# Output of tiles 3 to 6 on three pairs of half-filled banks, with attention running on into it, and a second set of temporaries

## The chip, the cores and the metric

One core of one Trainium2 chip. The metric is device time in microseconds (us). The kernel before took 848.38 us (median of 3 runs, 846.76 to 848.47).

## The reference

Attention within chunks of 64 tokens, for 8 batches, 8 heads and 576 tokens of 64 values, and behind it a two-layer feed-forward network with a quadratic ReLU:

```python
scores = scale * np.matmul(q_c, k_c.transpose(0, 1, 2, 4, 3))
scores = scores - np.max(scores, axis=-1, keepdims=True)
attn = np.exp(scores)
attn = attn / (np.sum(attn, axis=-1, keepdims=True) + 1e-09)
out = np.matmul(attn, v_c)
...
h = x @ w_in
g = np.where(pos, h, np.where(neg, 0.0, (h + beta) ** 2 / (4.0 * beta)))
return (g @ w_out).astype(np.float32)
```

x has 4608 tokens of 512 values, w_in is 512 x 2048 and w_out 2048 x 512, all in float32.

## The kernel before, in words

The tokens are cut into 9 tiles of 512. Every float32 operand of a matmul is split into a high and a low part of a rounded type (F32R), and a product is taken as three: high by high, high by low, low by high.

Tiles 0 to 2 run as plain products (`ffn_in`, line 607, and `ffn_out`, line 643), 16 steps a tile. While they run, two other things are made for the tiles behind them. `combine_weights` makes, for each of 8 pairs of blocks of w_in, the sums of a Strassen scheme with seven products, and `combine_out` does the same for w_out. Both work in four temporaries named `tmp`; from there the sums go to DRAM as `combos` (line 826) and `sums` (line 974) over the queue of GpSimd (POOL). The lists `WEIGHTS` and `SUMS_AT` say at which step of tiles 1 and 2 each pair has its turn; three pairs of w_out are not in the list, and `combine_out` is called for them while tiles 3 and 4 already run.

Tiles 3 to 8 run two at a time, as 3 and 4, 5 and 6, 7 and 8, each pair of tiles in two halves. In the hidden half, `whole_last` runs 56 products (`product`, line 891) of 6 matmuls of 512 columns, on the PSUM banks h0, h1, o0 and o1. In the output half, `both_out` runs 7 rounds, P1, P2, P6, P7, P4, P5, P3, of 8 products each (line 1101). A product there covers four blocks of 128 tokens. Before the change, each block has a bank for itself: rounds P1, P6, P4 and P3 take the banks o2, o3 and the pair `ps_a`, the other rounds take h0, h1, o0 and o1. The rounds in `wide` (P1, P6 and P4) make high by both halves of the factor in one matmul of 512 columns and add a second one of 256, 8 matmuls in all; the two halves of the bank are added when it is read. The other rounds use three matmuls of 256 columns per block, 12 in all. For the last pair of tiles nothing of this is changed.

Each product takes its weights from a ring of tiles in SBUF, `RING` places of 256 KB, which POOL's queue fills in the order of use (lines 864 and 869). A place is filled again when its product is done.

Attention of the later tiles is cut into 36 turns, 4 a tile. A burst is the value products of turn n and the score products of turn n + 2 (lines 487 and 465), both on the bank pair `ps_a`. Between them lies the softmax of the turn: VectorE (DVE) takes the maximum (line 521), ScalarE (ACT) the exponentials (line 530), DVE the division and a transposition (line 570), and eight small DMAs, four on SP's and four on POOL's queue, bring the result to `aT` (line 562), which the value products read two bursts later. `BURSTS` says before which of the 56 products of a hidden half a burst is placed. q, k and v of later turns are loaded over SP's queue (lines 382 and 398).

The order on each engine is not that of the code. `Plan` collects all operations with an estimated duration, and places them by readiness and turn; each engine then works its list in order and waits where an operand is late. So a late operand holds back what stands behind it on the same engine.

Of the kernel before, what the change touches and what calls it, by code (L numbers as in the profile page):

```python
# [133 lines left out]
def kernel(  # L134
# [540 lines left out]
    RING = 12  # L675
# [106 lines left out]
    def combine_weights(p):  # L782
        js = (2 * p, 2 * p + 1)
        keys = [[f"wi{j}_{n}" for n in range(2)] for j in js]
        (k1, w1), (k12, s12), (k2, w2), (k34, s34) = tmp_bufs

        def kc(ap):
            return ap.rearrange("p (i two f) -> p two i f", i=2, two=2)

        def two(ap, n):  # L790
            return ap[:, cols(n)].rearrange("p (i f) -> p i f", i=2)

        for j, ks, key, w in zip(js, keys, (k1, k2), (w1, w2)):
            dve(0.6, ALU.add, fixed(w), lambda j=j: weight["wi", j][:, 0, :].bitcast(F32),
                lambda j=j: weight["wi", j][:, 1, :].bitcast(F32), ks, (key,))
        a11, a12, a21 = kc(w1)[:, 0], kc(w1)[:, 1], kc(w2)[:, 0]
        a22 = kc(w2)[:, 1]
        dve(0.34, ALU.add, fixed(two(s12, 0)), fixed(a21), fixed(a22), (k2,), (k12,))
        dve(0.34, ALU.subtract, fixed(two(s12, 1)), fixed(two(s12, 0)), fixed(a11), (k1,), (k12,))
        dve(0.34, ALU.subtract, fixed(two(s34, 0)), fixed(a11), fixed(a21), (k1, k2), (k34,))  # L800
        dve(0.34, ALU.subtract, fixed(two(s34, 1)), fixed(a12), fixed(two(s12, 1)), (k1, k12), (k34,))
        for hkey, hi, key, ap in ((k1, w1, k12, s12), (k2, w2, k34, s34)):
            act_copy(0.52, fixed(hi.bitcast(F32R)), fixed(ap), (key,), (hkey,))
            dve(0.6, ALU.subtract, fixed(ap.bitcast(F32R)), fixed(ap), fixed(hi), (hkey,), (key,))
# [7 lines left out]
        def of_stage(n, h):  # L812
            return lambda: tmp_pairs[n][:, :, cols(h)].rearrange("p x (i f) -> p x i f", i=2)

        for r, src, reads in (
            (0, of_block(0, 0), (*keys[0], k12)), (1, of_block(0, 1), (*keys[0], k12)),
            (6, of_block(1, 1), (*keys[1], k12)),
            (2, of_stage(0, 1), st[0]), (3, of_stage(0, 0), st[0]),
            (5, of_stage(1, 0), st[1]), (4, of_stage(1, 1), st[1]),
        ):  # L820
# [117 lines left out]
    BURSTS = range(2, 46, 6)  # L938
# [17 lines left out]
    def combine_out(p):  # L956
        js = (2 * p, 2 * p + 1)
        keys = [[f"wo{j}_{n}" for n in range(2)] for j in js]
        (k1, w1), (k12, s12), (k2, w2), (k34, s34) = tmp_bufs
        for j, ks, key, w in zip(js, keys, (k1, k2), (w1, w2)):  # L960
            dve(0.6, ALU.add, fixed(w), lambda j=j: weight["wo", j][:, 0, :].bitcast(F32),
                lambda j=j: weight["wo", j][:, 1, :].bitcast(F32), ks, (key,), ahead=LATER)
        a11, a21, a12, a22 = (fixed(w[:, cols(n)]) for w in (w1, w2) for n in range(2))
        s1, s2, s3, s4 = (fixed(w[:, cols(n)]) for w in (s12, s34) for n in range(2))
# [4 lines left out]
        for hkey, hi, key, ap in ((k1, w1, k12, s12), (k2, w2, k34, s34)):  # L969
            act_copy(0.52, fixed(hi.bitcast(F32R)), fixed(ap), (key,), (hkey,), ahead=LATER)  # L970
            dve(0.6, ALU.subtract, fixed(ap.bitcast(F32R)), fixed(ap), fixed(hi), (hkey,), (key,), ahead=LATER)
        for n, name in enumerate(SUMS):
            def send(n=n, name=name):
                nc.gpsimd.dma_start(
                    out=sums[name, p].bitcast(F32), in_=tmp_pairs[n // 2][:, :, cols(n % 2)]
# [73 lines left out]
    def both_out(t, wide, then=None):  # L1049
# [8 lines left out]
        banks = {name: main if name in ("P1", "P6", "P4", "P3") else side for name in OUT_ORDER}  # L1058
        alone = ("P1", "P2", "P7", "P5", "P3")
# [11 lines left out]
        def operand_of(name, p):  # L1071
# [4 lines left out]
            act_copy(0.52, h, ap, (skey,), (hkey,))  # L1076
            dve(0.6, ALU.subtract, l, ap, plain(h), (skey, hkey), (lkey,))
# [35 lines left out]
        def pairs_of(name, half):  # L1113
            if banks[name] is side:
# [156 lines left out]
    def back(t, g):  # L1271
# [11 lines left out]
        ("x0",), ("x1",), ("x2",), ("x3", "x4"), ("x5", "x6"), ("x7", "x8"), ("x9", "x10"),  # L1283
        ("x11", "ring1"), ("ring2", "ring3"),
# [8 lines left out]
    SUMS_AT = (0, 16, 18, 20, 23)  # L1293
    WEIGHTS = (2, 4, 7, 9, 12, 14, NF + 10, NF + 12)
# [17 lines left out]
    for t in range(ALONE + 1):  # L1312
        for j in range(NF):
# [17 lines left out]
            if step in WEIGHTS:  # L1331
                combine_weights(WEIGHTS.index(step))
            if step in SUMS_AT:
                combine_out(SUMS_AT.index(step))
# [4 lines left out]
            if t == ALONE and j < len(HANDED):  # L1339
                hand_lot("wi", j, F32R, *HANDED[j])  # L1340
# [13 lines left out]
    for n, (key, _) in enumerate((*gh_bufs, *gl_bufs)):  # L1354
        take(f"ring_{key}", key, [P, T], F32R, (key,), (f"ring_{key}",))

    turns = [(n, n + 2) for n in range((ALONE + 3) * NP, ALL - 2)] + [(ALL - 2, None), (ALL - 1, None)]
    for t in range(ALONE + 1, NTILE, 2):
        if t > ALONE + 1:
            move_blocks()  # L1360
        for n, (p, name) in enumerate(alternating(0, NQ)):
            if n in BURSTS and turns:
                burst(*turns.pop(0))
# [73 lines left out]
```

## Time and profile before

| | |
|---|---|
| median of 3 runs | 848.38 us |
| the profiled execution | 848.42 us |
| its span, first to last instruction | 846.6 us |
| TensorE (PE) busy | 816.9 us, 96% |
| DVE busy | 665.0 us, 79% |
| ACT busy | 540.2 us, 64% |
| mean granted TensorE clock | 0.988 |

PE is busy nearly all the time, so what is of interest is where it is not, and where its clock is not full. The span lies in these stretches: tiles 0 to 2 up to about 327 us, the hidden half of tiles 3 and 4 to about 433, their output half to 518, the hidden half of tiles 5 and 6 to about 602 and their output half to 681, and the last pair of tiles to the end.

### The profile page before, as it was taken

How to read it: one execution, taken by the hardware profiler on the slowest of the kernel's cores; microseconds unless marked ns; L12 is line 12 of the kernel's file. 1: busy time of each engine (PE TensorE's matmuls, PEld its weight loads, DVE VectorE, ACT ScalarE, POOL GpSimd, SP SyncE). 2: the span in 40 equal slices, each digit the busy share in tenths (PEclk: the TensorE clock that was granted, in tenths of full speed). 3: DMA queues.
4: the chain of work that ended last, by engine and by line, in shares of the span. 5: the costliest groups of instructions: out<-in, count | busy, mean ns of one | idle time of the engine just before them, and what ended most of it. 6: DMA issues, size and time to landing. Idle time of an engine off the chain costs nothing.

```text
span 846.6 us, 18141 instructions
## 1 busy us (share of the span) xinstructions
PE 816.9 (96%) x6272; PEld 692.0 (82%) x6272; DVE 665.0 (79%) x1163; ACT 540.2 (64%) x1299; POOL 343.6 (41%) x606
## 2 busy tenths in 40 slices
PE   8999999999999999888699999999999999999998
PEld 8877788888878888666579999777899998888887
DVE  4999997877988885967489976867898755579962
ACT  5789885556676674857495545877855446677440
POOL 2233334354443554645343333545433334333330
PEclk9999999999999999989799999999999999999999
DMA  9999946676786997999986668986667675566762
GB/s 226 246 299 295 290 129 197 177 235 188 191 226 152 244 250 218 257 223 251 225 229 184 209 210 236 257 233 206 185 197 198 209 237 196 191 194 188 213 194 93
DMA packets 245354, 181.58 MB, mean 214 GB/s; under 512 B 192656, under 2 KB 210576, under 8 KB 245264
## 3 DMA queue, kind: packets, MB, share of 16 engines
q0 software_dynamic: 40640, 122.72, 46.0%
q1 hardware_dynamic: 202512, 57.18, 29.7%
q8 instruction: 50, 0.82, 0.4%
q10 hardware_dynamic: 2112, 0.52, 0.3%
q14 instruction: 40, 0.33, 0.1%
HBM read 133.17 MB, written 38.80 MB: 203 GB/s over the span
## 4 chain that ended last, share of the span: by engine, by line
PE 54%; DMA 8%; DVE 3%; ACT 3%; issue 2%; SPq 2%; POOL 0%; DVEq 0%; ACTq 0%; POOLq 0%
PE ps_o L1101 14%; PE ps_o L891 9%; PE ps_a L1101 8%; PE ps_h L891 7%; PE ps_h L1101 6%; PE ps_o L643 5%; PE ps_h L607 4%; DMA k_sb<-in_k_dram 2%; ACT e L530 1%; DMA sums_P<-tmp 1%; DVE new_wi L922 1%; SPq L382 1%; DMA v_sb<-in_v_dram 1%; PE ps_a L487 1%; DMA aT<-e 1%
## 5 line engine op out<-in xcount | busy, mean ns | idle before, releaser
L607 PE MATMUL ps_h<-xh,parts 128*128 128x512 f32 x384 | 130.0, 397 | 2.3 <-DVE parts L350 1.7
L724 ACT CAST new_wi<-new_wi 128x512 fp32r<-128x512 f32 x146 | 89.3, 620 | 67.0 <-PE ps_o L1101 34.6
L728 DVE TENSOR_TENSOR new_wi<-new_wi,new_wi 128x512 fp32r<-128x512 f32 (+1 forms) x186 | 120.3, 683 | 13.1 <-ACT new_wi L724 12.6
L643 PE MATMUL ps_o<-parts,gh 128*128 128x512 f32 x384 | 118.7, 390 | 0.4 <-DVE tmp L657 0.4
L607 PEld LDWEIGHTS ps_h<-xh,parts 128*128 128x128 f32 x384 | 71.9, 188 | 19.1 <-DVE parts L350 2.6
L643 PEld LDWEIGHTS ps_o<-parts,gh 128*128 128x128 f32 x384 | 71.8, 188 | 15.7 <-DVE tmp L657 0.8
L643 PE MATMUL ps_o<-parts,gl 128*128 128x512 f32 x192 | 74.8, 390 | 0.7 <-DVE gl L628 0.7
L864 POOL DMA_DIRECT2D new_wi<-sums_P x84 | 45.0, 536 | 68.2 <-PE ps_a L1101 28.9
L869 POOL DMA_DIRECT2D new_wi<-combos x84 | 45.4, 542 | 66.2 <-PE ps_o L891 27.6
L562 POOL DMA_DIRECT2D aT<-e x96 | 48.3, 511 | 50.6 <-issue 15.8
L1101 PE MATMUL ps_o<-new_wi,new_wi 128*128 128x256 f32 (+1 forms) x380 | 68.0, 309 | 0.0
L922 DVE SCALAR_TENSOR_TENSOR new_wi<-h,new_wi 128x512 f32<-128x512 f32 x62 | 41.9, 684 | 25.1 <-ACT new_wi L921 25.0
L891 PE MATMUL ps_o<-new_wi,new_wi 128*128 128x512 f32 x234 | 60.2, 399 | 0.0
L1101 PEld LDWEIGHTS ps_o<-new_wi,new_wi 128*128 128x128 f32 x380 | 53.9, 190 | 4.1
L530 ACT ACTIVATE e<-ps_a,mx 128x64 f32<-128x64 f32 x168 | 49.9, 325 | 8.8 <-DVE mx L526 6.2
L918 ACT ACTIVATE new_wi<-h 128x512 f32<-128x512 f32 x62 | 39.4, 638 | 21.5 <-DVE h L912 21.5
L891 PEld LDWEIGHTS ps_o<-new_wi,new_wi 128*128 128x128 f32 x234 | 44.2, 192 | 9.8 <-ACT snaps L724 0.3
L921 ACT ACTIVATE new_wi<-new_wi 128x512 f32<-128x512 f32 x84 | 51.4, 633 | 1.1
L607 PE MATMUL ps_h<-x_parts,parts 128*128 128x512 f32 x128 | 49.9, 390 | 0.0
L626 ACT CAST gh<-r 128x512 fp32r<-128x512 f32 x48 | 30.0, 626 | 28.0 <-PE ps_o L643 14.1
L891 PE MATMUL ps_h<-new_wi,new_wi 128*128 128x512 f32 x186 | 47.7, 391 | 0.0
L487 PEld LDWEIGHTS ps_a<-aT,v_sb 64*64 64x64 f32 x1056 | 20.8, 139 | 28.0 <-issue 19.2
(238 smaller groups left out, 2088.8 us busy)
## 6 DMA issues: line engine op xcount, KB each, us to landing
new_wi<-combos POOLq DMA_DIRECT2D x84, 256.0 KB, 4.2
new_wi<-sums_P POOLq DMA_DIRECT2D x84, 256.0 KB, 3.2
words<-in_moe_w_in_dram SPq DMA_DIRECT2D x16, 512.0 KB, 7.7
words<-in_moe_w_out_dram SPq DMA_DIRECT2D x16, 512.0 KB, 6.4
sums_P<-tmp POOLq DMA_DIRECT2D x32, 256.0 KB, 4.2
combos<-tmp POOLq DMA_DIRECT2D x32, 256.0 KB, 3.6
v_sb<-in_v_dram SPq DMA_DIRECT2D x60, 128.0 KB, 4.6
q_sb<-in_q_dram SPq DMA_DIRECT2D x112, 64.0 KB, 4.3
```

The source lines that it names most:

```text
L530: nc.scalar.activation(out=e3[:, n, :], in_=sc[:, n // 4, n % 4, :], func=AF.Exp, bias=mx[:, n, :], scale=SCALE, accum_out=sm[:, n, :],)
L562: queues[queue].dma_start(out=aT[b:b + Q, to], in_=x[a:a + Q, of])
L607: nc.tensor.matmul(out=ps, lhsT=weight["wi", j][:, half, kc * P:(kc + 1) * P], rhs=x, start=(kc == 0 and i == 0), stop=(kc == KC - 1 and i ...
L643: nc.tensor.matmul(out=acc, lhsT=x[:, cols], rhs=weight["wo", j][:, half, :], start=(j == 0 and i == 0), stop=(j == NF - 1 and i == 2),)
L724: "act", cost, lambda: nc.scalar.copy(out=out(), in_=src()), reads, writes, ahead=ahead
L728: plan.add("dve", cost, lambda: nc.vector.tensor_tensor(out=out(), in0=one(), in1=two(), op=op), reads, writes, port=True, ahead=ahead)
L864: plan.add("pool", 0.55, lambda: nc.gpsimd.dma_start(out=ap().bitcast(F32), in_=sums[name, p].bitcast(F32).rearrange("p x f -> p (x f)")), ...
L869: plan.add("pool", 0.55, lambda: nc.gpsimd.dma_start(out=ap().bitcast(F32), in_=combos[d][:, n, :].bitcast(F32)), (f"dram{d}_{n}",), (key, ...
L891: nc.tensor.matmul(out=ps, lhsT=w()[:, at:at + P], rhs=y(), start=name in FRESH and i == 0 and k == 0, stop=i == 1 and k == 2, skip_group_ ...
L921: plan.add("act", 0.52, lambda: nc.scalar.square(out=now(r), in_=now(r)), (), (rkey,), ahead=50)
L922: plan.add("dve", 0.6, lambda: nc.vector.scalar_tensor_tensor(out=now(r), in0=h(), scalar=1.0, in1=now(r), op0=ALU.max, op1=ALU.min), (hke ...
L1101: nc.tensor.matmul(out=into, lhsT=x()[:, block], rhs=factor, start=first and k == 0, stop=p == NQ - 1 and k == len(steps) - 1, skip_group_ ...
```

## The change

In the output halves of tiles 3 to 6 no round is wide. Two blocks of 128 tokens share a bank, each on 256 of its 512 columns, so that a round needs two banks. The rounds go over three pairs of banks: (o2, o3), (h0, h1) and (o0, o1). The pair `ps_a` is left to attention.

`BURSTS` places a burst every 9 products instead of every 6, and counts on into the output half: two of the eight bursts now lie there, before the fourth product of P1 and the fifth of P2.

`combine_weights` and `combine_out` can work in a second set of temporaries, `alt0` and `alt1`, which lie in the places of the first two blocks of w_in once tile 2 has used them; every second call from step 18 on uses it. Two more turns of `combine_out` are earlier: six pairs are in `SUMS_AT`, at steps 0, 6, 12, 18, 20 and 23, and two calls are left for tiles 3 and 4. In `combine_weights` the sends from the temporaries now come before those from the blocks. The ring has 10 places instead of 12; two of its pairs of places are gone and the buffers `r` take one pair's part, which come free only when tile 2's hidden layer is done.

```diff
-    RING = 12
+    RING = 10
...
+    def stage_of(again):
+        if again:
+            some = [(f"alt{n}_{i}", part_of(f"alt{n}", i)) for n in range(2) for i in range(2)]
+            return *some, [lambda n=n: held[f"alt{n}"] for n in range(2)]
+        return *((key, fixed(ap)) for key, ap in tmp_bufs), [fixed(pair) for pair in tmp_pairs]
...
-        if k >= 4:
-            key = f"ring_{(gh_bufs, gl_bufs)[n][k - 4][0]}"
+        if k >= 2:
+            key = f"ring_{(gh_bufs, gl_bufs, r_bufs)[k - 2][n][0]}"
...
-    BURSTS = range(2, 46, 6)
+    BURSTS = range(5, 72, 9)
...
+        if not last:
+            thirds = o_banks[2:], h_banks, o_banks[:2]
+            banks = {name: thirds[n] for name, n in zip(OUT_ORDER, (0, 1, 0, 2, 0, 1, 2))}
...
+            soon = 200 if name == "P1" and p < 2 else 0
...
-                    acc, block = banks[name][n][1], slice(n * P, (n + 1) * P)
+                    block = slice(n * P, (n + 1) * P)
+                    acc = banks[name][n][1] if last else banks[name][n // 2][1][:, cols(n % 2)]
...
-                        first = name in alone and p == 0
+                        first = name in alone and p == 0 and (last or n % 2 == 0)
...
+                between(len(alternating(0, NQ)) + NQ * OUT_ORDER.index(name) + p)
...
-    SUMS_AT = (0, 16, 18, 20, 23)
-    WEIGHTS = (2, 4, 7, 9, 12, 14, NF + 10, NF + 12)
+    SUMS_AT = (0, 6, 12, 18, 20, 23)
+    WEIGHTS = (2, 4, 8, 10, 14, 21, 26, 28)
+    AGAIN = sorted(step for step in (*SUMS_AT, *WEIGHTS) if step > 17)[::2]
...
+    def between(n):
+        if n in BURSTS and turns:
+            burst(*turns.pop(0))
...
-                if p % 2 and p < 2 * (NQ - len(SUMS_AT)):
-                    combine_out(len(SUMS_AT) + p // 2)
+                if p in (1, 4):
+                    combine_out(len(SUMS_AT) + p // 4, p > 1)
...
-            both_out(t, ('P1', 'P6', 'P4'), lambda raws=raws: pieces_of(raws))
+            both_out(t, then=lambda raws=raws: pieces_of(raws))
```

On PE, where tiles 3 and 4 go over from the hidden to the output half, before the change. Line 891 is a product of the hidden half, line 1101 one of the output half; `ps_o23` is the bank pair o2, o3.

```order
L891 MATMUL ps_o1_140<-new_wi2_3_2700,new_wi8_9_3154 128x512 x3
L891 MATMUL ps_o1_140<-new_wi6_7_3009,new_wi8_9_3154 128x512 x3
L1101 MATMUL ps_o23_137<-ring_gh0_3674,new_wi4_5_2873 128x512
L1101 MATMUL ps_o23_137<-ring_gh0_3674,new_wi4_5_2873 128x256
...
L1101 MATMUL ps_a_138<-ring_gh0_3674,new_wi4_5_2873 128x512
L1101 MATMUL ps_a_138<-ring_gh0_3674,new_wi4_5_2873 128x256
```

The same place after it; lines 899 and 1114 are the two lines' new numbers, 487 and 465 are a burst.

```order
L899 MATMUL ps_o_139<-new_wi_3_2703,ring_gh_3704 128x512 x3
L899 MATMUL ps_o_139<-new_wi_7_3031,ring_gh_3704 128x512 x3
L899 MATMUL ps_o_140<-new_wi_5_2891,ring_gh_3733 128x512 x3
L899 MATMUL ps_o_140<-new_wi_9_3187,ring_gh_3733 128x512 x3
L1114 MATMUL ps_o_137<-ring_r_3681,new_wi_4_2817 128x256 x12
L487 MATMUL ps_a<-aT_78,v_sb_72 64x64 x16
L465 MATMUL ps_a<-kT_75,qT_74 64x64 x16
L1114 MATMUL ps_o_137<-ring_r_3693,new_wi_7_3031 128x256 x12
```

A product of P1 was eight matmuls of two widths on four banks and is now twelve of 256 columns on two banks, and a burst on `ps_a` stands between two of them.

On POOL's queue, at the start of the hidden half of tiles 3 and 4, before the change; line 869 fills a place of the ring, line 974 sends sums of a pair (here pair 5) from `tmp` to DRAM, line 562 moves attention weights.

```order
L869 DMA new_wi_9_3154<-combos_109 128x512
L562 DMA aT_78<-e_76 32x256 x4
L869 DMA ring_gh_3674<-combos_112 128x512
L974 DMA sums_P_5_193<-tmp_135 256x1x256
L869 DMA ring_gl_3675<-combos_110 128x512
L974 DMA sums_P_5_169<-tmp_135 256x1x256
L869 DMA ring_gh_3703<-combos_111 128x512
L869 DMA ring_gl_3704<-combos_112 128x512
L974 DMA sums_P_5_177<-tmp_136 256x1x256
L974 DMA sums_P_5_201<-tmp_136 256x1x256
```

After it, from the last sends of tile 2 on; line 982 is 974's new number, 877 that of 869, and `new_wi_0` and `new_wi_1` are the second set of temporaries.

```order
L982 DMA sums_P_7_195<-new_wi_0_2541 256x1x256
L982 DMA sums_P_7_171<-new_wi_0_2541 256x1x256
L982 DMA sums_P_7_179<-new_wi_1_2611 256x1x256
L982 DMA sums_P_7_203<-new_wi_1_2611 256x1x256
L562 DMA aT_78<-x_80 32x256 x4
L562 DMA aT_79<-e_77 32x256 x4
L877 DMA ring_r_3681<-combos_104 128x512
L877 DMA new_wo_2_2729<-combos_107 128x512
L877 DMA ring_r_3693<-combos_105 128x512
L877 DMA ring_gh_3704<-combos_104 128x512
L877 DMA ring_gl_3705<-combos_105 128x512
```

Twelve sends of sums (pairs 5, 6 and 7) stood among the ring's fills of this half. Now those of pairs 5 and 7 stand ahead of its fills, and the four of pair 6 come some twenty rows further down.

## Rows read from the trace of the kernel before

**Rows 1.** The page: head.

```profile
span 846.6 us, 18141 instructions
```

**Rows 2.** Four stretches: length, PE, PEld, DVE, ACT, POOL busy, PEclk, DMA share, GB/s.

```profile
222.00:327.00 105.00, 104.61 (x927) 85.14 (x926) 88.67 (x175) 70.04 (x220) 47.39 (x81) 1.00 0.81 209
327.00:433.00 106.00, 89.28 (x825) 71.71 (x824) 75.22 (x146) 71.75 (x224) 52.66 (x96) 0.90 0.95 246
433.00:518.00 85.00, 84.31 (x595) 78.84 (x595) 75.65 (x128) 48.01 (x85) 31.82 (x61) 1.00 0.68 200
518.00:602.00 84.00, 81.80 (x763) 65.66 (x762) 59.69 (x108) 63.34 (x186) 40.35 (x77) 1.00 0.85 233
```

**Rows 3.** Waits of PE, 327 to 433 us: total, times, longest.

```profile
PE ps_a L487 <- DMA aT<-e: 9.4, 2, 7.7
PE ps_a L487 <- DMA aT<-x: 3.8, 1, 3.8
PE ps_a L487 <- DMA q_sb<-in_q_dram: 1.0, 1, 1.0
PE ps_h L891 <- DVE new_wi L922: 0.9, 1, 0.9
PE ps_h L891 <- DVE h L912: 0.8, 1, 0.8
PE ps_o L891 <- DVE new_wi L922: 0.8, 1, 0.8
```

**Rows 4.** Stretches of one burst and three products each, columns as in Rows 2.

```profile
371.82:377.09 5.27, 5.27 (x84) 4.22 (x82) 5.00 (x10) 4.95 (x21) 4.87 (x9) 1.00 1.04 237
363.92:371.82 7.90, 7.90 (x82) 6.62 (x83) 3.28 (x7) 2.38 (x5) 0.57 (x1) 0.66 0.68 143
387.31:395.38 8.07, 7.27 (x83) 5.83 (x83) 7.13 (x13) 5.01 (x20) 3.25 (x7) 0.79 0.82 217
415.56:423.18 7.62, 7.62 (x82) 6.44 (x83) 2.56 (x5) 1.81 (x3) 1.11 (x2) 0.68 0.60 115
```

**Rows 5.** The chain of waits, 340 to 440 us: start, length, what.

```profile
349.05 5.71 DMA sums_P<-tmp
354.76 0.71 ACT e L530 x5
...
359.25 4.42 DMA aT<-x
...
363.92 1.39 PE ps_a L487 x29
```

**Rows 6.** DMA queues and two issue lines, 327 to 433 us.

```profile
q0 software_dynamic: 6031, 17.56, 51.8%
q1 hardware_dynamic: 44331, 8.34, 42.7%
...
sums_P<-tmp POOLq DMA_DIRECT2D x12, 256.0 KB, 6.2
...
new_wo<-combos POOLq DMA_DIRECT2D x7, 256.0 KB, 6.8
```

**Rows 7.** Rounds P6 and P5 of tiles 3 and 4, and 40 us around.

```profile
460.68:471.98 11.30, 11.30 (x66) 9.80 (x65) 11.30 (x21) 6.00 (x10) 4.29 (x8) 1.00 0.79 229
494.81:506.32 11.51, 11.51 (x98) 11.51 (x97) 10.87 (x19) 6.00 (x10) 4.29 (x8) 1.00 0.77 231
440.00:480.00 40.00, 40.00 (x277) 37.17 (x277) 40.00 (x70) 24.19 (x42) 15.21 (x29) 1.00 0.69 197
```

**Rows 8.** Waits of PE, 518 to 602 us: total, times, longest.

```profile
PE ps_a L487 <- ACT snaps L724: 1.3, 1, 1.3
PE ps_a L487 <- DMA aT<-e: 0.4, 1, 0.4
PE ps_o L891 <- DVE new_wi L922: 0.3, 1, 0.3
```

**Rows 9.** A group by line, DVE, 327 to 433 us: busy us, mean ns.

```profile
L521 DVE TENSOR_REDUCE mx<-ps_a 128x8 f32<-128x512 f32 x8 | 5.5, 686 | 11.5 <-ACT more L724 7.9 <-PE ps_a L465 3.6
```

More of the change, by code (lines that the diff above doesn't have):

```diff
@@ L793, in combine_weights @@
         for j, ks, key, w in zip(js, keys, (k1, k2), (w1, w2)):
-            dve(0.6, ALU.add, fixed(w), lambda j=j: weight["wi", j][:, 0, :].bitcast(F32),
+            dve(0.6, ALU.add, w, lambda j=j: weight["wi", j][:, 0, :].bitcast(F32),
                 lambda j=j: weight["wi", j][:, 1, :].bitcast(F32), ks, (key,))
-        a11, a12, a21 = kc(w1)[:, 0], kc(w1)[:, 1], kc(w2)[:, 0]
-        a22 = kc(w2)[:, 1]
-        dve(0.34, ALU.add, fixed(two(s12, 0)), fixed(a21), fixed(a22), (k2,), (k12,))
@@ L799, in combine_weights @@
-        dve(0.34, ALU.subtract, fixed(two(s12, 1)), fixed(two(s12, 0)), fixed(a11), (k1,), (k12,))
-        dve(0.34, ALU.subtract, fixed(two(s34, 0)), fixed(a11), fixed(a21), (k1, k2), (k34,))
-        dve(0.34, ALU.subtract, fixed(two(s34, 1)), fixed(a12), fixed(two(s12, 1)), (k1, k12), (k34,))
+        a11, a12, a21, a22 = (kc(w, n) for w in (w1, w2) for n in range(2))
+        dve(0.34, ALU.add, two(s12, 0), a21, a22, (k2,), (k12,))
+        dve(0.34, ALU.subtract, two(s12, 1), two(s12, 0), a11, (k1,), (k12,))
@@ L954, in keep_factor, with combine_out @@
                  moving=0.8, ahead=LATER)
-    def combine_out(p):
+    def combine_out(p, again=False):
         js = (2 * p, 2 * p + 1)
         keys = [[f"wo{j}_{n}" for n in range(2)] for j in js]
-        (k1, w1), (k12, s12), (k2, w2), (k34, s34) = tmp_bufs
+        (k1, w1), (k12, s12), (k2, w2), (k34, s34), pairs = stage_of(again)
         for j, ks, key, w in zip(js, keys, (k1, k2), (w1, w2)):
-            dve(0.6, ALU.add, fixed(w), lambda j=j: weight["wo", j][:, 0, :].bitcast(F32),
+            dve(0.6, ALU.add, w, lambda j=j: weight["wo", j][:, 0, :].bitcast(F32),
                 lambda j=j: weight["wo", j][:, 1, :].bitcast(F32), ks, (key,), ahead=LATER)
-        a11, a21, a12, a22 = (fixed(w[:, cols(n)]) for w in (w1, w2) for n in range(2))
-        s1, s2, s3, s4 = (fixed(w[:, cols(n)]) for w in (s12, s34) for n in range(2))
+        a11, a21, a12, a22 = (part(w, n) for w in (w1, w2) for n in range(2))
+        s1, s2, s3, s4 = (part(w, n) for w in (s12, s34) for n in range(2))
         dve(0.34, ALU.add, s1, a21, a22, (k1, k2), (k12,), ahead=LATER)
@@ L974, in send @@
                 nc.gpsimd.dma_start(
-                    out=sums[name, p].bitcast(F32), in_=tmp_pairs[n // 2][:, :, cols(n % 2)]
+                    out=sums[name, p].bitcast(F32), in_=pairs[n // 2]()[:, :, cols(n % 2)]
                 )
@@ L1047, in take_low, with both_out @@
         plan.add("pool", 0.0, emit, (), (key,))
-    def both_out(t, wide, then=None):
+    def both_out(t, wide=(), then=None):
         last = then is None
@@ L1113, in pairs_of @@
         def pairs_of(name, half):
+            if not last:
+                return [((key,), lambda ap=ap: ap.rearrange("p (n d) -> p n d", n=2), b, None)
+                        for b, (key, ap) in enumerate(banks[name])]
             if banks[name] is side:
@@ L1331 @@
             if step in WEIGHTS:
-                combine_weights(WEIGHTS.index(step))
+                combine_weights(WEIGHTS.index(step), step in AGAIN)
             if step in SUMS_AT:
-                combine_out(SUMS_AT.index(step))
+                combine_out(SUMS_AT.index(step), step in AGAIN)
             if t == 0 and j >= 8:
@@ L1339 @@
             if t == ALONE and j < len(HANDED):
-                hand_lot("wi", j, F32R, *HANDED[j])
+                hand_lot("wi", j, F32 if j < 2 else F32R, *HANDED[j])
                 if j == 2:
@@ L1361 @@
         for n, (p, name) in enumerate(alternating(0, NQ)):
-            if n in BURSTS and turns:
-                burst(*turns.pop(0))
+            between(n)
             if t == ALONE + 1 and name == "P1":
-                if p % 2 and p < 2 * (NQ - len(SUMS_AT)):
-                    combine_out(len(SUMS_AT) + p // 2)
+                if p in (1, 4):
+                    combine_out(len(SUMS_AT) + p // 4, p > 1)
                 place_blocks(p)
```

38 lines of the change are left out of this document (21 added, 17 removed).

## The prediction

> **What bounds the kernel now.** I read the page's head first, then a table of stretches, then PE's waits in the stretch that stands out, then the chain of waits there. The span is 846.6 us [rows 1], and the profiled execution took 848.42 us, so 1.8 us lie around the span; the median of the runs is 848.38 us, so what is summed against the profiled execution holds for the median as well.
>
> The table of stretches [rows 2] shows a PE that is full in the tiles before (104.61 of 105 us) and in the output half of tiles 3 and 4 (84.31 of 85), and one stretch that is not: 327 to 433 us, the hidden half of tiles 3 and 4, with 89.28 of 106 us at a mean granted clock of 0.90. It is also the stretch with the fullest DMA engines, a share of 0.95 against 0.68 behind it. So the question is what the change does to this stretch, and what it costs in the others.
>
> PE's waits there [rows 3] sum to 9.4 + 3.8 + 1.0 + 0.9 + 0.8 + 0.8 = 16.7 us, and 14.2 us of them are value products that wait for a load or for the moves of the attention weights. Behind each of the three long waits the clock is at its lower level for a while. Four stretches of equal work, a burst and three products, give its price [rows 4]: undisturbed it takes 5.27 us at clock 1.00; behind the waits it takes 7.90, 8.07 (with a wait of 0.8 in it) and 7.62 us. That is 2.6 + 2.0 + 2.4 = 7.0 us more. So this stretch loses 16.7 + 7.0 = 23.7 us, and PE's work in it is 106 - 23.7 = 82.3 us.
>
> Why are the moves late? The chain [rows 5] shows one case: a send of sums from the temporaries took 5.71 us to land, then ACT's exponentials went on, then the move took 4.42 us, and then PE started. ACT had stood still, since the next copy into those temporaries was ahead of the exponentials in its order. The queues show the wider cause [rows 6]: POOL's queue kept the 16 engines for 51.8% of 106 us, which is 54.9 us for 17.56 MB or 67 transfers of 256 KB (0.82 us each), and SP's queue for 42.7%, which is 45.3 us for 8 turns of attention (5.7 us each). Together 100.2 us of transfers against 82.3 us of PE work: the stretch asks for more than its length.
>
> The Trainium skill (Trainium Kernel Development and Optimization, Key Constraints) says that DMAs from the SP, ACT and POOL queues all run on the same 16 engines. By that rule the two shares add up, as I do here; if each queue had engines of its own, neither 54.9 nor 45.3 us would fill 82.3 us, and the waits would have to be latency. The trace agrees with the rule in so far as the mean share of 0.95 is their sum.
>
> **The change part by part.**
>
> *Fewer transfers beside tiles 3 and 4's hidden half.* Of the 12 sends of sums [rows 6] four are left there, by the order on POOL's queue: 8 x 0.82 = 6.6 us less. Two of eight bursts move to the output half: 2/8 x 45.3 = 11.3 us less. That leaves 100.2 - 6.6 - 11.3 = 82.3 us, by chance just PE's work. The move of a turn also gets more time: it is read two bursts later, and two bursts were 12 products apart and are now 18; at about 1.4 us a product (a round of eight takes 11.30 us [rows 7]) that is 25 us instead of 17. And the sums of pair 7 use the second temporaries, so the pattern of the chain can come up once, not three times. What stays lost: nothing as the lower bound; as the upper bound of this mechanism, 82.3 us of transfers at the rate that the full stretch had, 100.2 us in 106, take 87.1 us, 4.8 us over PE's work. The stretch 518 to 602 us, with a DMA share of 0.85 on the mean, still loses 2.0 us [rows 8]. I take 4, near the upper end, since the load is uneven within the stretch: 23.7 - 4 = 19.7 us gained.
>
> *Tiles 5 and 6's hidden half.* The same spacing, with 2.0 us to gain at most [rows 8]; I take 1.0.
>
> *No wide rounds.* A wide round of 8 products takes 11.30 us and one of 12-matmul products 11.51 us, both with PE full [rows 7]: 0.21 us a round, and six rounds change (P1, P6, P4, twice), so 1.3 us more, on PE's path and hidden by nothing. The weights of a product are loaded beside the matmul before; in the row of 12 matmuls the loads are as long as PE (11.51 of 11.51 us), which is why more of them show.
>
> Of this the Trainium skill (TensorE: Matmul & The Clock Gate, Back-to-back issue gap) gives about 2.5 ns of fixed cost for each further matmul; an estimate from that is 192 more matmuls x 2.5 ns = 0.5 us. The rows say 1.3 us, and the measurement decides; the forecast would be 0.8 us lower by the Trainium skill.
>
> *Reading the banks.* Six times two adds of 128x512 on DVE go, three times per output half. They stood beside PE's next round, so they free DVE and no time on PE's path by themselves.
>
> *Attention in the output half.* DVE is the engine to watch: 40.00 of 40 us between 440 and 480 us [rows 7], with PE full only because DVE's splits run some products ahead. A turn's softmax costs DVE five instructions of the size of the maximum, which takes 0.69 us [rows 9]: 3.5 us, so two turns bring 6.9 us; the four adds of P1 and P6 that go in that span take 2.8 us away. Net 4.1 us in a stretch where DVE has no gap. What covers it: after 484 us DVE has room (75.65 of 85 us in the whole half [rows 2]). If the lead is used up, PE waits for at most these 4.1 us; if it is not, nothing. In tiles 5 and 6 the two bursts there have no scores any more, so no softmax. I take 1.5 us, nearer to nothing, since PE waits there only once before. PE queues nothing else behind such a wait that could go on.
>
> *The ring's 10 places.* A load starts 10 products ahead, some 14 us, and the slowest kind lands within 6.8 us on the median in the full stretch [rows 6]. At the start of the stretch six of the places come free only with the end of tile 2's work, but four products are loaded before. The bound is one late load at each of the three starts, 0 to 3 us. The two earlier turns of `combine_out` and the shifted ones of `combine_weights` go into tiles 1 and 2, where PE had no wait and DVE 88.67 of 105 us [rows 2]; one more set of some 4 us fits. Both together: 0 to 4 us, I take 0.5.
>
> *The sum:* -19.7 - 1.0 + 1.3 + 1.5 + 0.5 = -17.4 us, 848.4 - 17.4 = 831 us.
>
> **The rivals.**
>
> 1. *The DMA engines still bound the stretch.* The 82.3 us of transfers are just PE's work, so any that I counted too low, or the pair's four sends together with the ring's first fills, bring back waits of several us, each with its slow clock behind it. For it speaks that the share is 0.95 with no slack; against it that 518 to 602 us loses little at 0.85. With half of the loss left, 11.9 us: 831 + 7.9 = 839 us.
>
> 2. *Everything goes.* No wait is left in either hidden half and DVE's lead holds: 848.4 - 23.7 - 2.0 + 1.3 = 824 us. For it speaks that the three long waits hang on single late moves; against it that short waits for DVE [rows 3] are no matter of DMA.
>
> 3. *Slower: the wait is the softmax's way through three engines in order, not traffic.* Then each burst waits as before wherever it stands, 23.7 us stay lost, and the two that move into the output half take their waits along (16.7 / 8 = 2.1 us each, in a half that lost nothing) on top of the 1.3 and 4.1 us: 848.4 + 4.2 + 5.4 = 858 us. It decides if the moves are issued too late although the transfers are short. For it speaks the ACT step in the chain [rows 5]; against it that in that chain two of the steps ahead of PE are landings of 5.71 and 4.42 us.
>
> 4. *No change: what the moves gain, the ring loses.* With 10 places and POOL's queue still full, PE waits for weights where it waited for `aT`. That gives about 848 us. Against it: not one of the waits in the fullest stretch is for a ring load [rows 3].
>
> **How the numbers follow.** My forecast (826 to 836 us) has 0.53, rival 1 0.20, rival 2 0.13, rival 3 0.08 and rival 4 0.06. A measurement of this kernel can tell a change of over 0.2% (1.7 us) from none. Faster are the forecast and rivals 1 and 2, of which I give 0.01 to no change: 0.85 faster, 0.07 the same, 0.08 slower. The range reaches from a little below rival 2 to rival 1 with all bounds of the unknown costs: 822 to 843 us.
>
> **What the profile after would show.** Right: the hidden half of tiles 3 and 4 is about 20 us shorter for the work in it, its clock is near 1.00, at most one wait for `aT` over 1 us is left, and the DMA share in the output half has risen from 0.68 towards 0.8. A round of P1, P6 or P4 takes 11.5 us. The DVE term is wrong if PE waits for splits in P1 or P2 for more than 3 us, the ring's if PE waits at line 899 or 1114 for a load. The whole is wrong if the value products wait for `aT` as long as before.

## The result and the profile after

| | before | after |
|---|---|---|
| median | 847.57 us (4 runs, 846.68 to 848.47) | 826.70 us (4 runs, 825.11 to 829.03) |
| profiled execution, span | 848.42, 846.6 us | 825.11, 823.3 us |
| PE busy, mean clock | 816.9 us, 0.988 | 808.5 us, 1.000 |

The ratio is 0.9756 (0.9729 to 0.9783): the change takes 20.9 us off. The head of the page after, with its row of PE's granted clock:

```profile
span 823.3 us, 18510 instructions
...
PE 808.5 (98%) x6464; PEld 693.5 (84%) x6464; DVE 659.5 (80%) x1143; ACT 539.0 (65%) x1295; POOL 344.4 (42%) x606
...
PEclk9999999999999999999999999999999999999999
```

Stretches after: tiles 3 and 4's hidden half with most of P1, the rest of their output half, and round P6. The columns are those of [rows 2].

```profile
319.00:421.00 102.00, 99.51 (x867) 80.70 (x866) 77.95 (x139) 77.44 (x212) 52.53 (x98) 1.00 0.97 255
421.00:497.00 76.00, 76.00 (x685) 75.65 (x684) 66.75 (x115) 41.70 (x95) 31.83 (x60) 1.00 0.78 224
438.55:450.07 11.52, 11.52 (x99) 11.52 (x97) 11.49 (x22) 6.33 (x11) 6.32 (x12) 1.00 1.03 301
```

Waits of PE after, first 319 to 421 us, then 421 to 600 us:

```profile
PE ps_h L899 <- DVE h L920: 1.5, 1, 1.5
PE ps_o L899 <- DVE new_wi L930: 0.6, 1, 0.6
PE ps_h L899 <- DVE r L618: 0.3, 1, 0.3
PE ps_o L899 <- ACT h L724: 0.2, 1, 0.2
...
PE ps_h L899 <- DVE new_wi L930: 0.3, 1, 0.3
```

No wait for a transfer is left, and the slow clock behind such waits is gone. From the first hidden product to the end of tiles 3 and 4's output half the trace before takes 517.84 - 319.95 = 197.9 us and after 496.15 - 319.54 = 176.6 us, 21.3 us less. From there to the end it is 1.6 us less (328.76 and 327.15), and the start of the stretch 0.4 us earlier: together 23.3 us, the difference of the spans. The medians lie 20.9 us apart, since the traced execution after is the fastest of its four; sums from the two traces come out some 2 us high for that.

Yet the DMA engines are as full as before: a share of 0.97 over 102 us, in which PE works 99.5 us, against 0.95 with 16.7 us of waits [rows 2, 3]. So the DMA share does not say what went. What does are the moves of the attention weights. Here are their issues (line 562) before, on SP's queue and on POOL's: how many, their length in ns (least, median, most), when the first and the last started, who waited for them, and how long they took to land.

```profile
L562 SPq DMA_DIRECT2D aT<-x x8: 517/558/585, 357.4 to 396.4; - x8
...
who waited for it (us, times):
  PE ps_a L487: 13.2, 3
...
DMA to landing us min/median/max: 1.8/4.0/8.9
```

```profile
L562 POOL DMA_DIRECT2D aT<-x x8: 496/500/528, 351.0 to 392.8; - x8
...
who waited for it (us, times):
  POOL new_wi L869: 2.0, 3
...
DMA to landing us min/median/max: 2.8/4.5/7.9
```

Each turn's moves are shared between the two queues. All 13.2 us that PE waited for `aT` ended with SP's half, none with POOL's, though POOL's took no less time to land. SP's half was late because SP issued it late: the first `aT<-x` stood ready at 350.69 us (DVE's transposition, 349.99 + 0.70), POOL issued its half at 351.0, SP at 357.4. What SP did meanwhile is in its timeline before (start, length, issues); SP works in order, and the loads of q and k for a later turn stood ahead:

```profile
345.33 1.11 SPq L398 DMA_DIRECT2D v_sb<-in_v_dram  x2
346.54 6.24 SPq L382 DMA_DIRECT2D q_sb<-in_q_dram  x4
352.88 4.43 SPq L382 DMA_DIRECT2D k_sb<-in_k_dram  x4
357.42 2.42 SPq L562 DMA_DIRECT2D aT<-x  x4
359.93 1.10 SPq L398 DMA_DIRECT2D v_sb<-in_v_dram  x2
```

The rows follow each other almost without a gap: this turn took 359.93 - 345.33 = 14.6 us, and eight q and k issues 10.7 of them. After the change the same view reads:

```profile
338.34 1.92 SPq L382 DMA_DIRECT2D q_sb<-in_q_dram  x4
340.36 2.23 SPq L382 DMA_DIRECT2D k_sb<-in_k_dram  x4
346.47 2.46 SPq L562 DMA_DIRECT2D aT<-e  x4
349.03 2.12 SPq L398 DMA_DIRECT2D v_sb<-in_v_dram  x2
352.53 3.23 SPq L382 DMA_DIRECT2D q_sb<-in_q_dram  x4
```

There are gaps now (342.6 to 346.5 us, 351.2 to 352.5). Between 327 and 423 us SP's waits sum to 13.7 of 96 us before and to 36.2 after. The longest of before, then the two longest of after:

```profile
SPq L382 <- DMA k_sb<-in_k_dram: 3.3, 2, 3.0
```

```profile
SPq L382 <- DVE qT L441: 8.8, 3, 4.6
SPq L398 <- PE ps_a L487: 7.8, 3, 2.9
```

After, SP waits for the readers of q and of v to give their places back: it is ahead of its turns. I call the time from the end of a turn's transposition to SP's first issue of its move the lag. Before, the seven turns from 340 to 410 us have lags of 1.0, 6.7, 7.2, 0.9, 3.8, 9.0 and 7.4 us, a mean of 5.1; after, six turns have 0.0, 3.7, 2.7, 1.1, 0.7 and 1.0, a mean of 1.5. The landing itself has not become shorter: the median over all `aT` transfers is 4.2 us before (327 to 433 us) and 4.7 after (319 to 421 us).

### The profile page after: what moved, and what is told of

Same layout as the page of the kernel before. It is cut to its first block, busy times and chain, and to the rows that moved or that the text cites. A ratio compares the mean times of both kernels' runs of the same rounds, so it can differ in the third digit from the quotient of the medians.

```text
span 823.3 us, 18510 instructions
## 1 busy us (share of the span) xinstructions
PE 808.5 (98%) x6464; PEld 693.5 (84%) x6464; DVE 659.5 (80%) x1143; ACT 539.0 (65%) x1295; POOL 344.4 (42%) x606
## 4 chain that ended last, share of the span: by engine, by line
PE 64%; DVE 12%; DMA 9%; ACT 5%; issue 5%; SPq 3%; POOL 2%; DVEq 0%; ACTq 0%; POOLq 0%
PE ps_o L1114 19%; PE ps_o L899 11%; PE ps_h L899 11%; PE ps_h L1114 8%; PE ps_o L643 5%; PE ps_h L607 5%; PE ps_a L1114 3%; DMA aT<-x 2%; DVE tmp L728 2%; DMA sums_P<-parts 2%; ACT e L530 1%; DVE new_wi L728 1%; DVE r L618 1%; DMA combos<-tmp 1%; PE ps_a L487 1%
## 5 line engine op out<-in xcount | busy, mean ns | idle before, releaser
L724 ACT CAST new_wi<-new_wi 128x512 fp32r<-128x512 f32 x154 | 94.4, 628 | 66.3 <-PE ps_o L1114 33.7
L728 DVE TENSOR_TENSOR new_wi<-new_wi,new_wi 128x512 fp32r<-128x512 f32 (+2 forms) x192 | 123.5, 676 | 15.6 <-ACT new_wi L724 15.2
L643 PEld LDWEIGHTS ps_o<-parts,gl 128*128 128x128 f32 x192 | 36.0, 188 | 8.9 <-DVE gl L628 1.4
L957 POOL DMA_DIRECT2D sums_P<-parts x24 | 17.8, 788 | 57.7 <-DVE parts L350 57.5
L628 DVE TENSOR_TENSOR gl<-r,gh 128x512 fp32r<-128x512 f32 x48 | 32.8, 685 | 7.8 <-ACT gh L626 7.1
L618 DVE SCALAR_TENSOR_TENSOR r<-ps_h,r 128x512 f32<-128x512 f32 x48 | 32.5, 681 | 7.2 <-ACT r L617 7.1
L728 DVE TENSOR_TENSOR new_wi<-new_wi 128x512 f32<-128x512 f32 (+2 forms) x60 | 37.4, 635 | 0.3
L530 ACT ACTIVATION_READ_ACCUMULATOR e<-ps_a,mx 128x1 f32 x168 | 37.1, 221 | 0.0
L1114 PE MATMUL ps_o<-new_wo,new_wi 128*128 128x256 f32 (+1 forms) x244 | 34.8, 292 | 0.0
L1114 PE MATMUL ps_o<-ring_gh,new_wi 128*128 128x256 f32 (+1 forms) x244 | 34.6, 292 | 0.0
```

What stands on the lines that cost most here:

```text
L530: nc.scalar.activation(out=e3[:, n, :], in_=sc[:, n // 4, n % 4, :], func=AF.Exp, bias=mx[:, n, :], scale=SCALE, accum_out=sm[:, n, :],)
L618: plan.add("dve", 0.6, lambda: nc.vector.scalar_tensor_tensor(out=r, in0=ps, scalar=1.0, in1=r, op0=ALU.max, op1=ALU.min), (pkey,), (rkey,))
L643: nc.tensor.matmul(out=acc, lhsT=x[:, cols], rhs=weight["wo", j][:, half, :], start=(j == 0 and i == 0), stop=(j == NF - 1 and i == 2),)
L724: "act", cost, lambda: nc.scalar.copy(out=out(), in_=src()), reads, writes, ahead=ahead
L728: plan.add("dve", cost, lambda: nc.vector.tensor_tensor(out=out(), in0=one(), in1=two(), op=op), reads, writes, port=True, ahead=ahead)
L1114: nc.tensor.matmul(out=into, lhsT=x()[:, block], rhs=factor, start=first and k == 0, stop=p == NQ - 1 and k == len(steps) - 1, skip_group_ ...
```

## The experiments

Each kernel ran beside the kernel before on the same chip; the ratios are to that. "The change" is the kernel after.

**1. The change with bursts six apart** (`e1_six_apart`).

```diff
-    BURSTS = range(5, 72, 9)
+    BURSTS = range(2, 46, 6)
```

> The changed kernel with its bursts again before the products 2, 8, ... 44 of the hidden half, 6 apart and none in the output half; the moved sums, the second temporaries, the narrow rounds and the ring of 10 stay. Traffic theory (the stretch asked for more transfers than it is long): two turns or 11.3 us of transfers come back, 82.3 + 11.3 = 93.6 us against 82.3 us of PE work, so 10 to 17 us of the gain are lost again: 837 to 844 us, with waits for aT in the hidden half of tiles 3 and 4. Sums theory (the sends of sums and their temporaries held ACT and DVE back, the spacing is idle): no change, 825 to 829 us. Distance theory (the spacing alone made the gain, whatever the traffic): all of it is lost, 845 to 850 us.

Measured: 841.82 us, 0.9947 (0.9918 to 0.9976). PE's longest wait in total, 325 to 430 us, and the stretch:

```profile
PE ps_a L487 <- DMA q_sb<-in_q_dram: 10.5, 3, 5.1
```

```profile
330.00:424.00 94.00, 80.96 (x802) 65.39 (x801) 65.22 (x124) 65.74 (x213) 43.65 (x82) 0.95 0.99 242
```

With the sums moved but the bursts as close as before, the waits and the slow clock are back. The view names loads of q, but line 487 reads `aT` and `v_sb`. It names the transfer on whose semaphore a count came last, and in this program a move and a load of q that is issued after it often have one semaphore. The moves that these three products read were issued 1.8, 6.3 and 6.6 us after their transposition, and the last part of each landed 0.1 to 0.3 us before its product began: these were waits for SP's half of the move, as before the change. So the spacing and place of the bursts carry some 15 of the 21 us, all else in the change some 5. The time lies in the range of the traffic theory, and outside the other two.

**2. The steps of the sums as before, and one set of temporaries** (`e2_sums_as_before`, `e3_one_set`). The first takes the lists, the calls and the one set of temporaries from before:

```diff
-    SUMS_AT = (0, 6, 12, 18, 20, 23)
-    WEIGHTS = (2, 4, 8, 10, 14, 21, 26, 28)
-    AGAIN = sorted(step for step in (*SUMS_AT, *WEIGHTS) if step > 17)[::2]
+    SUMS_AT = (0, 16, 18, 20, 23)
+    WEIGHTS = (2, 4, 7, 9, 12, 14, NF + 10, NF + 12)
+    AGAIN = ()
...
-                if p in (1, 4):
-                    combine_out(len(SUMS_AT) + p // 4, p > 1)
+                if p % 2 and p < 2 * (NQ - len(SUMS_AT)):
+                    combine_out(len(SUMS_AT) + p // 2)
```

The second takes away the second set alone:

```diff
-    AGAIN = sorted(step for step in (*SUMS_AT, *WEIGHTS) if step > 17)[::2]
+    AGAIN = ()
...
-                    combine_out(len(SUMS_AT) + p // 4, p > 1)
+                    combine_out(len(SUMS_AT) + p // 4)
```

> The changed kernel with the steps of combine_weights and combine_out as before, three calls of combine_out in the hidden half of tiles 3 and 4, and one set of temporaries; bursts 9 apart, output on three pairs of banks and the ring of 10 stay. Traffic theory: 8 sends or 6.6 us of transfers come back, 88.9 us against 82.3, so 6 to 11 us are lost: 833 to 838 us. Sums theory: nearly all of the gain is lost, 842 to 850 us. Distance theory: at most 2 us are lost, 826 to 829 us.

> The changed kernel with the second set of temporaries not used, every sum in tmp again; the steps stay as in the change. The four sends of pair 7 fall back into the hidden half of tiles 3 and 4. Traffic theory: 3.3 us of transfers more, 0 to 4 us lost, 827 to 831 us. Sums theory: the copies into tmp wait for the sends again and hold ACT's exponentials back, 6 us or more lost, 833 us or more. Distance theory: nothing lost, 825 to 828 us.

Measured: 830.23 us, 0.9778 (0.9743 to 0.9812), and 827.11 us, 0.9757 (0.9731 to 0.9783). The earlier sums are worth some 2 to 4 us, with intervals that overlap the change's; the second set is worth nothing that can be measured. The sums theory is out by both; the first time lies between the ranges of the other two. PE's second longest wait with the sums as before, 319 to 440 us, behind one of 2.4 us for DVE:

```profile
PE ps_o L1114 <- DMA ring_gl<-sums_P: 1.8, 1, 1.8
```

Here the ring does wait. The lag on SP's queue is back at 5.8 us on the mean of six turns, and still no move is waited for: at nine products apart a turn has the time. That is the reading that fits; no run shows it by itself.

**3. Narrow rounds alone, in the kernel before** (`e4_narrow_alone`).

```diff
-            both_out(t, ('P1', 'P6', 'P4'), lambda raws=raws: pieces_of(raws))
+            both_out(t, (), lambda raws=raws: pieces_of(raws))
```

> The kernel before with no wide round in the output halves of tiles 3 to 6, on the banks as before; nothing else is changed. By the rows of before six rounds take 11.51 instead of 11.30 us, 1.3 us more: 849 to 850 us against 848. If the cost of a further matmul were only about 2.5 ns, 0.5 us more. A rival: DVE's adds that go let its splits run further ahead, and as the only wait of this half was for a split (0.7 us), the whole is even.

Measured: 849.14 us, 1.0016 (0.9996 to 1.0035, 12 runs): +1.4 us, the forecast's size, but not told apart from no change.

**4. Lighter loads of q and k, in the kernel before.** In `e5_light_loads` they are taken by rows, with half the packets in half the issues; `e5b_light_same_issues` has the same packets in as many issues as before, by `load_quarters` in place of `load_rows`, which makes two DMAs of each. Both bring other values of q and k for tiles 3 to 8. The first one's edit:

```diff
-                lambda load=load, dst=dst, src=src: load(eng, dst, src, t, g),
+                lambda load=load_rows if load == load_blocks and t > 2 else load, dst=dst, src=src: load(eng, dst, src, t, g),
```

> The kernel before, with q and k of tiles 3 to 8 fetched in runs of 256 bytes instead of 128 (whole rows of a head instead of half rows, so their values stand in the wrong places and the output is not the reference's); the order on every engine, the sums, the temporaries and the spacing of 6 stay. As many bytes in half as many packets. Traffic theory: q and k are most of a turn's 5.7 us of transfers; a cut of 1.5 to 2 us a turn takes 12 to 16 us off the 100.2 us of the stretch, to 84 to 88 us, and most of its waits go: 828 to 838 us. Distance theory (two bursts of 12 products are too near for the softmax's way through the engines, whatever the traffic): 844 to 850 us.

> As e5_light_loads, but with as many DMAs on SP's queue as the kernel before (four each for q and k, 64 KB each, now in runs of 256 bytes); the values of q and k stand in the wrong places again, so the output is not the reference's. Traffic theory: the packets are what counts, 832 to 838 us as in e5_light_loads. Rival (SP's queue issues too slowly, and e5 gained because it had half as many issues): 843 to 848 us.

Measured: 834.41 us, 0.9864 (0.983 to 0.9898), and 842.42 us, 0.9934 (0.9908 to 0.996). Each is compared with the kernel before on its own chip: of 12.4 us that the light loads bring, 5.4 are the packets and the rest the number of issues. The first time lies in the range of the traffic theory; the second lies far above the 832 to 838 us of that theory, and just under its rival's range. The stretch with half the issues, and the wait for `aT` there:

```profile
327.00:418.00 91.00, 82.38 (x786) 65.17 (x778) 71.22 (x141) 68.29 (x218) 49.13 (x90) 0.96 1.06 270
```

```profile
PE ps_a L487 <- DMA aT<-e: 3.0, 1, 3.0
```

The DMA share rose to 1.06 while the waits for `aT` fell from 13.2 to 3.0 us. So at 0.95, with 13.2 us of waits, the 16 engines had not been at their limit. SP's timeline there, and of the kernel with as many issues as before:

```profile
353.53 1.43 SPq L368 DMA_DIRECT2D q_sb<-in_q_dram  x2
355.48 1.49 SPq L368 DMA_DIRECT2D k_sb<-in_k_dram  x2
359.12 2.49 SPq L562 DMA_DIRECT2D aT<-e  x4
```

```profile
369.06 3.29 SPq L378 DMA_DIRECT2D q_sb<-in_q_dram  x4
372.45 6.43 SPq L378 DMA_DIRECT2D k_sb<-in_k_dram  x4
380.11 3.44 SPq L572 DMA_DIRECT2D aT<-e  x4
```

With half the issues the lag is 0.4 us on the mean of eight turns; with as many as before it is 3.8, and PE waits 9.1 us for `aT`. So with the same bytes and packets, the number of issues on SP's queue decides some 7 us.

**5. Heavier loads, in the change** (`e6_heavy_loads`, `e6b_heavy_few_issues`). q is fetched once more into a buffer in DRAM, in four more issues a turn; or k, in two issues of 1024 pieces of 128 bytes each, behind the turn's own loads.

```diff
-                lambda load=load, dst=dst, src=src: load(eng, dst, src, t, g),
+                lambda load=load, dst=dst, src=src, n=n: (load(eng, dst, src, t, g), load(eng, spare[turn(t, g)], src, t, g) if n == "q" and turn(t, g) >= 20 else None),
```

```diff
+                for i in range(2 if n == "k" and turn(t, g) >= 22 else 0):
+                    eng.dma_start(out=spare[turn(t, g)][:, :, i * Q:(i + 1) * Q],
+                                  in_=src[BATCH[t], 2 * g:2 * g + 2, :T, i * Q:(i + 1) * Q])
```

> The changed kernel with the q of each turn from 20 on fetched a second time, in the same packets, into a DRAM buffer that nothing reads; the order of all other work stays. Traffic theory: some 2 us more for each of six turns, about 12 us on top of 82.3 in the hidden half of tiles 3 and 4; the stretch asks for more than its length again, with waits for q or aT, and 8 to 16 us are lost: 835 to 843 us. Distance theory: with bursts 9 products apart the later landings still fit, 826 to 829 us.

> The changed kernel with k of each turn from 22 on fetched a second time into a DRAM buffer that nothing reads, in 2 DMAs behind the turn's own loads and not before turn 22, so that the stores of tile 2 don't wait behind them on SP's queue. 2048 further packets a turn; by the rows of before a packet on SP's queue keeps its engine 16.4 ns (45.3 us x 16 engines / 44331), so 2.1 us a turn, some 12 us in the hidden half of tiles 3 and 4. Traffic theory: 835 to 843 us, with waits for q, k or aT there. Rival (e6 lost its time to the stores behind 4 more issues a turn, not to traffic): 827 to 831 us.

Measured: 842.67 us, 0.9948 (0.9917 to 0.9979), and 991.01 us, 1.1687 (1.1643 to 1.1731). The first hit a number of the traffic theory in another way than that theory meant: the longest wait of PE was 7.7 us for `h` from DVE, which waited for tile 2's stores behind the extra issues on SP:

```profile
DVE tmp L729 <- DMA out_dram<-tmp: 9.9, 2, 7.1
```

So it does not tell the theories apart. The second lies far outside both of its ranges. Its stretch:

```profile
319.00:520.00 201.00, 133.92 (x1055) 111.98 (x1056) 96.94 (x175) 93.37 (x263) 57.86 (x108) 0.82 0.63 154
```

The longest wait of PE is 23.3 us for `h`, again behind tile 2's stores, which the later start was to spare. Beside it five bursts wait 48.9 us for `aT` (9.8 us on the mean), at a mean DMA share of 0.63. SP's timeline shows why; line 427 is the two copies, 568 the move. The last row is a burst on PE:

```profile
429.52 2.06 SPq L383 DMA_DIRECT2D q_sb<-in_q_dram  x4
431.68 2.61 SPq L383 DMA_DIRECT2D k_sb<-in_k_dram  x4
434.33 7.74 SPq L427 DMA_DIRECT2D spare<-in_k_dram  x2
442.18 10.48 SPq L568 DMA_DIRECT2D aT<-e  x4
452.76 1.08 SPq L399 DMA_DIRECT2D v_sb<-in_v_dram  x2
```

```profile
454.16 1.25 PE L493 MATMUL ps_a<-aT,v_sb 64*64 64x64 f32 x29 [11.28 <-DMA aT<-e]
```

SP issues almost without a gap, and a turn takes it 24.4 us (`v_sb` rows at 428.35 and 452.76). The burst starts 1.5 us after SP's last issue of its move, and 24.4 us after the burst before it, where bursts nine products apart take 13.7 us if PE doesn't wait. So PE goes at the pace of SP's queue here, with the DMA engines far from full. Why the move's four issues take 10.48 us behind the copies, and 2.42 us elsewhere, stays open.

**6. A ring of 8 in the change** (`e7_ring_of_8`).

```diff
-    RING = 10
+    RING = 8
```

> The changed kernel with a ring of 8 places, the buffers r not used for it. Traffic theory: a load then starts 8 products or 11 us ahead and lands in about 5 us; nothing waits for it but at the start of the hidden half of tiles 3 and 4: 827 to 830 us. Ring rival: if the ring's depth carries the DMA engines' load, PE waits for weights in that half: 833 us or more.

Measured: 831.46 us, 0.9825 (0.9791 to 0.986), 4.8 us over the change. PE's second longest wait, 319 to 430 us, behind one of 2.5 us for DVE:

```profile
PE ps_o L899 <- DMA ring_gh<-combos: 1.1, 1, 1.1
```

Depth begins to cost at 8; that 10 places cost nothing fits, but a ring of 12 in the change was not run. The time lies between the two ranges.

**7. Spacing alone, and other spacings.** `e8_before_seven_apart` changes one line of the kernel before, so that all eight bursts stay in the hidden half; `e10_seven_apart` and `e9_eleven_apart` change it in the change.

```diff
-    BURSTS = range(2, 46, 6)
+    BURSTS = range(2, 56, 7)
```

```diff
-    BURSTS = range(5, 72, 9)
+    BURSTS = range(5, 55, 7)
```

```diff
-    BURSTS = range(5, 72, 9)
+    BURSTS = range(5, 85, 11)
```

> The kernel before with its bursts 7 products apart instead of 6, at 2, 9, ... 51, all still in the hidden half; nothing else is changed. Traffic theory: the same transfers in the same stretch, so it loses nearly the same, 843 to 848 us. Distance theory: two bursts are 14 products apart instead of 12, a third of the way to 18; a third of what the spacing made is gained, 841 to 843 us or less.

> The changed kernel with its bursts 7 apart, at 5, 12, ... 54, all in the hidden half. Traffic theory: the transfers are those of e1_six_apart, but spread over 49 products and the end of the half instead of 42; 835 to 841 us, between e1_six_apart (841.8) and the change. Distance theory: 14 products between two bursts, a third of the way from 841.8 to 826.7, 837 us; the two theories differ little here, and what tells is whether PE's waits are for loads of q and k (traffic) or for aT alone (distance).

> The changed kernel with the bursts 11 products apart, from 5 to 82, so that three of the eight lie in the output half. Traffic theory: 5.7 us of transfers fewer in the hidden half, but what waits are left there are short ones for DVE; 0 to 1 us gained, unless DVE's splits of the rounds P1, P2 and P6 now come late: 825 to 829 us. Distance theory: the same.

Measured: 836.75 us, 0.9887 (0.9856 to 0.9918); 829.45 us, 0.9798 (0.977 to 0.9825); 826.74 us, 0.9773 (0.9741 to 0.9805). The first stretch of the kernel before at seven apart, and its longest wait:

```profile
327.00:421.00 94.00, 83.96 (x764) 66.96 (x762) 76.70 (x147) 71.55 (x224) 50.69 (x92) 0.96 1.00 265
```

```profile
PE ps_a L487 <- DMA q_sb<-in_q_dram: 6.3, 1, 6.3
```

This wait too has a load of q for its name and is one for a move. SP's issue of that move, and the burst that reads it:

```profile
355.75 3.10 SPq L562 DMA_DIRECT2D aT<-x  x4
```

```profile
363.90 1.25 PE L487 MATMUL ps_a<-aT,v_sb 64*64 64x64 f32 x29 [6.29 <-DMA q_sb<-in_q_dram]
```

The transposition had ended at 348.41 us, so the lag is 7.3 us, and the move's last part landed at 363.66.

One product more between bursts takes 11.0 us off the kernel before, although all eight bursts are still in the hidden half: the traffic theory had 843 to 848 us for it. Seven apart in the change is likewise faster than that theory's 835 to 841 us. With the change's other parts, seven apart comes within 2.7 us of nine; its waits, 319 to 425 us, name no load and no move, this one and one of 1.6 us for DVE ahead of four of 0.2 to 0.6 us:

```profile
PE ps_o L899 <- ACT snaps L724: 2.3, 1, 2.3
```

Eleven apart gives what nine gives. No kernel here beats the change.

## Why the prediction was right, and where not

**The place and the sign: right.** The gain is where it was put, in tiles 3 and 4's hidden half, by waits for `aT` and the slow clock behind them: 23.7 us before, 2.6 after, so 21.1 us. The clock is 1.00, no wait for `aT` is over 1 us, the share in the output half rose from 0.68 to 0.78.

**The first term: the size nearly, the mechanism not.** -19.7 us were forecast, with 4 us left for DMA traffic; 2.6 us are left, and all of them are waits for DVE and ACT. That the size came so near is no merit of the reason given: 23.7 us is what [rows 3] and [rows 4] show as lost, and any cause that took those waits away would have given it. The step that failed is "the stretch asks for more than its length", the sum of both queues' shares as what makes the moves late. The Trainium skill (Trainium Kernel Development and Optimization, Key Constraints) says that DMAs from the SP, ACT and POOL queues run on the same 16 engines; nothing here speaks against that, but it was the wrong limit. The share is 0.97 now with no wait for it; the kernel before gained 11.0 us with all eight bursts still in the hidden half; and light loads raised the share to 1.06 and took 12.4 us off.

What the runs put in its place is SP's queue, which issues 14 DMAs a turn in order, the move behind q and k. In the stretch before, SP issued for 96 - 13.7 = 82.3 of 96 us; a turn came every 12.5 us on the mean (SP's `v_sb` rows start at 345.33 and, six turns on, at 420.39), so it took SP 82.3 / 96 x 12.5 = 10.7 us. Bursts six products apart are 5.27 us [rows 4] and three products of some 1.4 us, together 9.5 us, apart if PE doesn't wait; at seven apart it is 10.9, at nine 13.7. By these means SP can't keep up at six and falls behind until PE waits for it, and from seven on it can. That fits the steps (841.8, 829.5, 826.7 and 826.7 us at 6, 7, 9 and 11 apart). The lag alone does not set the time: it was 4.3 us at seven apart and 5.8 with the sums as before, harmless since a turn had more products to pass before its move was read.

Both halves of this, issue (the light loads) and distance (the spacings), are held up by runs. The comparison of 9.5, 10.9 and 13.7 with 10.7 is weaker. The heavier loads of k bear it out: where a turn kept SP 24.4 us, bursts came 24.4 us apart. But with light packets in as many issues as before, the same working gives (96 - 28.6) / 96 x 12.4 = 8.7 us a turn, less than 9.5, and PE still waited 9.1 us for `aT`. There the longest wait, 6.6 us, was for the move at 380.11 us in the rows above, behind one issue of k that took 6.43 us. So a mean that fits does not rule out a single late turn, and more distance should help against that too, which no run tells apart. A kernel with the move ahead of the q and k loads on SP's queue would be the direct test; it was not tried. By their numbers alone the runs don't decide: the traffic theory's ranges hold the times of six apart, one set, light loads with half the issues, the second fetch of q, and eleven apart. What speaks against it are the times with the sums as before, at seven apart (twice) and with light loads in as many issues as before, all outside its ranges, and the shares beside the waits.

**Which parts of it carry it.** The forecast gave credit to fewer sends of sums (6.6 us of transfers), bursts moved out (11.3 us) and the second temporaries, which were to end the pattern of the chain [rows 5]. That chain was read too far: it crosses from SP's move to ACT by a wait of 0.3 us, here in SP's waits before, 345 to 366 us, which sum to 1.4 us:

```profile
SPq L562 <- ACT snaps L724: 0.3, 1, 0.3
```

For the rest of those 21 us SP was issuing, so it was its loads that held this move up and not ACT. The sums are worth 2 to 4 us, the second set nothing, and leaving the hidden half at most the 2.7 us between seven and nine apart. The longer way between a burst and the products that read its move (25 us instead of 17) stood in the prediction only as a remark, with no term of its own, and it carries most.

**Narrow rounds: right.** +1.3 us forecast; P6 takes 11.52 us (11.30 before [rows 7]), and the run alone gave +1.4 us, within its error. The 2.5 ns for each further matmul of the Trainium skill (TensorE: Matmul & The Clock Gate, Back-to-back issue gap) fall short here as they did in the rows. The Trainium skill gives them there in a formula for an isolated matmul, and says that in a stream with weight loads both set the spacing; the prediction took the formula without this. The trace agrees with the caution: the weight loads fill 11.52 of P6's 11.52 us.

**DVE in the output half: mis-sized.** +1.5 us taken, nothing measured: PE is busy 76.00 of 76 us, and there is no wait for DVE in 421 to 497 us. The lead held; DVE is at 66.75 of 76 us.

**Tiles 5 and 6, the ring:** -1.0 us forecast, -1.6 measured for all behind tiles 3 and 4 (waits 2.0 to 0.3, one more set of narrow rounds at 0.7 against it, the rest not resolved). The ring cost 0.5 in the sum and nothing is seen: no wait for a ring load, and 8 places do show one.

**The rivals.** The result lies 2.7 us over "everything goes" (824) and 4.3 under the forecast (831): DVE (1.5) and the ring (0.5) cost nothing that can be seen, and 2.6 us were left in place of the residue of 4, so that these three were 3.4 us too dear; the later tiles gave some 0.6 more. Rival 1 fell with its mechanism. Rival 3 is out in its result, but its condition, "the moves are issued too late although the transfers are short", was nearer to the cause than my forecast; the order was SP's, not ACT's, and so time between bursts cured it. Rival 4 is out.

## What to carry to other kernels

When a consumer waits for a DMA, look first at when it was issued, beside the time its data was ready and the other queue's half of the same transfer: a late issue is a matter of what stands ahead on that queue, and a full DMA share says nothing on it. Then compare the time that one turn keeps the queue with the distance between turns, since a few products more between them can be worth more than transfers taken away. And when a view names a transfer that the waiting instruction doesn't read, look up which one it reads and when that was issued.

## What the hardware showed

- The time to issue is not fixed: four q or k issues of 64 KB in pieces of 128 bytes took 1.92 us at best (after) and 6.24 us at worst (before) in the rows above, and the four issues of a move 2.42 us, but 10.48 behind two copies of 1024 pieces each. Whether it is the small packets or the busy engines that hold SP up is open.
- The mean share of the 16 DMA engines did not tell PE's waits for transfers: 0.95 stood beside 14.2 us of them (before), 0.99 beside 10.5 (six apart), 1.00 beside 6.3 (seven apart in the kernel before), 1.06 beside 3.0 (light loads), 0.97 beside none (after), and 0.63 beside some 10 us a burst (heavier loads of k).
